# Loading V of a sliding-window attention in 18-token runs and transposing it twice

## The chip, the cores and the metric

The kernel runs on one core of a Trainium2 chip. The metric is the device time of one execution in microseconds (us), lower is better. A run counts as slow when it is over 1.5% above the fastest of the same kernel; every ratio below compares fast runs alone, while a median quoted is of all runs of a kernel, and where a slow one is among them this is said. A profile is of a single execution, and its span is about 1.8 us shorter than that execution's time. The profile of the kernel before (441.0 us) is of one of its faster runs.

## The reference

Eight batches of eight heads, 576 tokens, head size 64. Causal attention over the last 64 tokens, then a spectral mixing layer whose 64 modes each multiply by two 512 x 512 weight matrices, then a channel product with a residual.

```python
def _attn_ref(q, k, v):
    scores = scale * np.matmul(q, k.transpose(0, 1, 3, 2))
    mask = (rel >= 0) & (rel < 64)
    ...
    return np.matmul(attn, v)

def _moe_ref(x, w_r, w_i, w_ch):
    X = np.fft.rfft(x, axis=1)
    Yr = einsum('bmd,mde->bme', Xr, w_r) - einsum('bmd,mde->bme', Xi, w_i)   # 64 modes
    Yi = einsum('bmd,mde->bme', Xr, w_i) + einsum('bmd,mde->bme', Xi, w_r)
    y = np.fft.irfft(Y, n=S, axis=1); u = x + y
    return u + np.maximum(u @ w_ch, 0.0)
```

The 128 weight matrices (1 MB each in float32) are most of what has to be read.

## The kernel before

Three stages follow each other: attention, in 36 windows of 8 query blocks; the modes, which stream the weights; and the output tail. Weights are prefetched during attention. There are two kinds of prefetch. 19 "early" weights have buffers of their own and can be loaded at any time. 14 "spares" are loaded into attention's own buffers (raw K, Q, V, the transposed K and Q, the V tiles) when attention has used them for the last time.

```python
    def load_qk(b):
        rk = rawp.tile([128, 2, RUN * D], BF16, name="rk")      # RUN = 18 tokens; rawp has 2 buffers of each
        rq = rawp.tile([128, 2, RUN * D], BF16, name="rq")
        for r, src in ((rk, k), (rq, q)):
            nc.gpsimd.dma_start(out=r, in_=src[b].rearrange("(x g) (p c) d -> (g p) x (c d)", g=4, c=RUN))

    def load_v(b):
        rv = rawp.tile([128, 9, 4, D], BF16, name="rv")
        vf = v[b].rearrange("(hp hl) t d -> hp (hl t) d", hl=2)
        for hp in range(4):                                     # four loads of 4-token runs
            nc.gpsimd.dma_start(out=rv[32 * hp:32 * hp + 32, ...].rearrange("r j c d -> r j (c d)"),
                                in_=vf[hp].rearrange("(j r c) d -> r j (c d)", j=9, r=32))
    # ... in transpose_units(b):
        def vpart(a, j0, j1):                                   # selection matmuls: V onto key partitions
            ...
            for c in range(4):
                for i in range(2):
                    hp = 2 * a + i; pp = slice(32 * hp, 32 * hp + 32)
                    nc.tensor.matmul(out=pss[i][:, 0:n, :], lhsT=pick[pp, c, :],
                                     rhs=rv[pp, j0:j1, c, :], start=(c == 0), stop=(c == 3))
            ...
        return [vpart(0, 0, 5), part(rk, kT, 0, True), part(rk, kT, 6, False),
                vpart(0, 5, 9), part(rk, kT, 12, True), part(rq, qT, 0, True),
                vpart(1, 0, 5), part(rq, qT, 6, False), part(rq, qT, 12, True),
                vpart(1, 5, 9)]
    # ... the attention loop: three units of batch b in each of four windows
        def unit(b, j):
            ...
            if j == NU - 1:                                     # all units of batch b are traced
                if b + 2 < B:
                    load(b + 2)                                 # K, Q, V of batch b + 2
                early(2)                                        # the next two early weights
                if b >= B - 2:
                    early(EARLY); spare_raw()
```

Each engine works its instructions off in a fixed order. On PE that order is the program's (it is pinned there); on the other engines the framework's scheduler chooses it when the kernel is built. All loads are issued by POOL, in one such order, and each waits for its buffer, so a load that waits holds up every load behind it.

The softmax here doesn't subtract the row's maximum and nothing guards it: scores larger than these inputs give would overflow.

## Time and profile before

The median was 444.94 us (442.81 to 447.34, 4 runs).

From the page of the kernel before: each row has 40 slices of the span, 11 us each. PE is the busy share in tenths, PEclk the granted clock of PE in tenths, DMA the busy share of the DMA engines, GB/s what they wrote.

```profile
span 441.0 us, 11418 instructions
...
PE   6999999948998665122268886988576685899994
...
PEclk9999999986998555555558899686765856699998
DMA  8999999999999999999999999999999999991787
GB/s 138 196 207 209 213 209 208 212 209 213 209 213 214 214 214 232 238 214 209 197 213 202 213 202 211 212 214 214 213 213 214 215 213 213 213 189 40 246 301 273
```

From the third slice to the 35th the rate stays between 197 and 215 GB/s, mostly at 208 or more; the one rise, to 238, is the load of w_ch, which keeps its four bytes. Loads cast float32 to bf16, so twice that is read. PE is nearly always busy in the first 12 slices (attention), about a third idle in the middle (modes wait for weights; 128 of the 200 us between 180 and 380 us are busy), busy again at the end (tail). So the DMA stream decides when the modes end, and PE decides the tail.

The same by stage (the busy microseconds of each engine in each stretch, then PE's granted clock, DMA share and GB/s; the DMA share sums the times of packets, and here it passes 1):

```profile
core 0: us, PE busy (x) PEld busy (x) DVE busy (x) ACT busy (x) POOL busy (x), PEclk, DMA share, GB/s
12.00:100.00 88.00, 77.61 (x1533) 46.90 (x1533) 52.88 (x103) 55.17 (x103) 32.50 (x53) 0.98 1.16 208
100.00:150.00 50.00, 44.05 (x798) 26.74 (x801) 24.67 (x48) 25.31 (x48) 11.75 (x21) 0.84 1.10 212
...
180.00:380.00 200.00, 127.97 (x1656) 94.35 (x1657) 61.80 (x128) 29.50 (x59) 40.69 (x77) 0.69 1.06 211
```

From the page's groups of instructions and its DMA issues (KB each, us from issue to landing):

```profile
L105 POOL DMA_DIRECT2D rv<-in_v_dram x32 | 20.0, 628 | 20.3 <-DMA wt<-in_moe_w_i_dram 5.0
...
L238 PEld LDWEIGHTS <-pick 32*128 32x128 bf16 x256 | 10.8, 93 | 15.4 <-DMA rv<-in_v_dram 6.8
...
rk<-in_k_dram POOLq DMA_DIRECT2D x8, 576.0 KB, 11.8
...
rv<-in_v_dram POOLq DMA_DIRECT2D x32, 144.0 KB, 11.3
```

V takes 32 issues of 144 KB where K takes 8 of 576 KB, and the selection weights are loaded into PE 256 times. From POOL's timeline, the loads of batch 4 (start, duration, and what ended the idle time before):

```profile
start us, us, engine line op out<-in xcount [idle before <-releaser]
41.93 0.73 POOL L97 DMA_DIRECT2D rk<-in_k_dram  x1 [6.57 <-PE pst L223]
42.65 0.56 POOL L121 DMA_DIRECT2D wt<-in_moe_w_i_dram  x1
43.20 0.54 POOL L121 DMA_DIRECT2D wt<-in_moe_w_r_dram  x1
46.34 0.71 POOL L97 DMA_DIRECT2D rq<-in_q_dram  x1 [2.59 <-PE pst L223]
47.64 2.46 POOL L105 DMA_DIRECT2D rv<-in_v_dram  x4 [0.60 <-PE psv_1054 L238]
```

K of batch 4 is issued at 41.93 us, Q at 46.34, V at 47.64. Three early weights were issued earlier, two stand between K and Q. PE first works on them at 64.3 us. From 20 us to the end of attention PE waits for a load for more than 1 us only once, for V of batch 6 (us in total, times, longest):

```profile
engine line waited for: us in total, times, longest us
PE psv_2252 L238 <- DMA rv<-in_v_dram: 6.7, 1, 6.7
```

### The profile page before, as it was taken

How to read it: one execution, taken by the hardware profiler on the slowest of the kernel's cores; microseconds unless marked ns; L12 is line 12 of the kernel's file. 1: busy time of each engine (PE TensorE's matmuls, PEld its weight loads, DVE VectorE, ACT ScalarE, POOL GpSimd, SP SyncE). 2: the span in 40 equal slices, each digit the busy share in tenths (PEclk: the TensorE clock that was granted, in tenths of full speed). 3: DMA queues.
4: the chain of work that ended last, by engine and by line, in shares of the span. 5: the costliest groups of instructions: out<-in, count | busy, mean ns of one | idle time of the engine just before them, and what ended most of it. 6: DMA issues, size and time to landing. Idle time of an engine off the chain costs nothing.

```text
span 441.0 us, 11418 instructions
## 1 busy us (share of the span) xinstructions
PE 328.7 (75%) x4989; PEld 218.9 (50%) x5002; DVE 187.8 (43%) x393; ACT 141.4 (32%) x269; POOL 129.2 (29%) x217
## 2 busy tenths in 40 slices
PE   6999999948998665122268886988576685899994
PEld 2455656525565565122146665755344353555552
DVE  6475666633764103108612323221134433345774
ACT  4566767733764001001113232222110110104553
POOL 8642442323121322101212112121122122113484
PEclk9999999986998555555558899686765856699998
DMA  8999999999999999999999999999999999991787
GB/s 138 196 207 209 213 209 208 212 209 213 209 213 214 214 214 232 238 214 209 197 213 202 213 202 211 212 214 214 213 213 214 215 213 213 213 189 40 246 301 273
DMA packets 38338, 92.49 MB, mean 210 GB/s; under 512 B 3472, under 2 KB 12688, under 8 KB 38288
## 3 DMA queue, kind: packets, MB, share of 16 engines
q0 software_dynamic: 33040, 82.32, 96.7%
q1 hardware_dynamic: 5248, 9.44, 6.0%
q8 instruction: 39, 0.64, 0.5%
q14 instruction: 11, 0.09, 0.1%
HBM read 163.58 MB, written 9.44 MB: 392 GB/s over the span
## 4 chain that ended last, share of the span: by engine, by line
DMA 46%; PE 28%; issue 18%; POOL 3%; ACT 3%; DVE 1%; POOLq 0%; ACTq 0%
DMA wt<-in_moe_w_r_dram 31%; DMA wt<-in_moe_w_i_dram 11%; DMA rv<-in_v_dram 4%; PE pso L318 3%; POOL wt L121 3%; PE psc L727 2%; PE pss_212 L378 2%; PE pst L223 2%; PE psu L745 2%; PE psx L340 2%; PE psy L505 1%; PE psy L500 1%; PE psc L733 1%; PE psu L740 1%; ACT et L300 1%
## 5 line engine op out<-in xcount | busy, mean ns | idle before, releaser
L505 PE MATMUL psy<-XQ,wt 128*128 128x16 bf16 x912 | 56.2, 191 | 47.1 <-DMA wt<-in_moe_w_i_dram 47.0
L500 PE MATMUL psy<-XQ,wt 128*128 128x16 bf16 x912 | 58.1, 191 | 34.6 <-DMA wt<-in_moe_w_r_dram 29.8
L121 POOL DMA_DIRECT2D wt<-in_moe_w_i_dram x57 | 30.7, 538 | 178.1 <-PE psy L505 154.6
L505 PEld LDWEIGHTS <-wt 128*128 128x128 bf16 x912 | 43.8, 104 | 58.4 <-DMA wt<-in_moe_w_i_dram 56.9
L500 PEld LDWEIGHTS <-wt 128*128 128x128 bf16 x912 | 44.3, 104 | 45.7 <-DMA wt<-in_moe_w_r_dram 36.3
L543 DVE CAST xT<-pxt 128x512 fp32r<-128x512 bf16 x36 | 23.4, 687 | 67.4 <-PE pxt L540 67.4
L546 PE MATMUL psz<-wch,xT 128*128 128x512 f32 x144 | 47.7, 477 | 1.0 <-DVE xT L543 1.0
L548 ACT CAST Z_3232<-psz 128x512 fp32r<-128x512 f32 x36 | 21.1, 587 | 76.0 <-PE psz L546 76.0
L121 POOL DMA_DIRECT2D wt<-in_moe_w_r_dram x57 | 30.9, 541 | 37.7 <-PE psy L505 13.9
L666 DVE TENSOR_TENSOR Z_3232<-pse,Z_3232 128x512 fp32r<-128x512 f32 x36 | 23.7, 688 | 34.0 <-PE pse L644 33.4
L546 PEld LDWEIGHTS psz<-wch,xT 128*128 128x128 f32 x144 | 30.4, 224 | 7.2 <-issue 0.8
L318 PEld LDWEIGHTS <-et 128*64 128x64 bf16 (+1 forms) x576 | 22.8, 111 | 14.8 <-issue 8.3
L755 POOL TENSOR_TENSOR ot<-ot,r 128x512 f32<-128x512 f32 x18 | 22.8, 1286 | 23.2 <-ACT Yb_5588 L59 13.3
L326 DVE TENSOR_TENSOR x_sb<-pso,rcp 128x640 bf16<-128x640 f32 x32 | 26.3, 822 | 0.9
L105 POOL DMA_DIRECT2D rv<-in_v_dram x32 | 20.0, 628 | 20.3 <-DMA wt<-in_moe_w_i_dram 5.0
L60 DVE CAST YT<-psy 128x256 fp32r<-128x256 f32 x6 | 2.5, 423 | 53.2 <-PE psy L505 53.2
L748 ACT ACTIVATE r<-psc 128x512 f32<-128x512 f32 x36 | 19.0, 601 | 10.2 <-PE psc L733 9.6
L238 PEld LDWEIGHTS <-pick 32*128 32x128 bf16 x256 | 10.8, 93 | 15.4 <-DMA rv<-in_v_dram 6.8
L59 ACT CAST YT<-psy 128x256 fp32r<-128x256 f32 x6 | 2.2, 374 | 49.5 <-DVE YT L60 49.5
L318 PE MATMUL pso<-vt_204,et 128*64 128x65 bf16 (+1 forms) x288 | 17.1, 204 | 0.0
L300 ACT ACTIVATE et<-pss_211 128x512 bf16<-128x512 f32 x24 | 14.3, 597 | 7.4 <-PE pss_212 L294 7.4
L318 PE MATMUL pso<-vt_205,et 128*64 128x65 bf16 (+1 forms) x288 | 16.1, 208 | 0.5 <-DVE x_sb L326 0.5
(334 smaller groups left out, 631.9 us busy)
## 6 DMA issues: line engine op xcount, KB each, us to landing
wt<-in_moe_w_r_dram POOLq DMA_DIRECT2D x57, 512.0 KB, 10.6
wt<-in_moe_w_i_dram POOLq DMA_DIRECT2D x57, 512.0 KB, 8.6
out_dram<-ot SPq DMA_DIRECT2D x32, 256.0 KB, 2.3
rk<-in_k_dram POOLq DMA_DIRECT2D x8, 576.0 KB, 11.8
rq<-in_q_dram POOLq DMA_DIRECT2D x8, 576.0 KB, 13.3
rv<-in_v_dram POOLq DMA_DIRECT2D x32, 144.0 KB, 11.3
qT<-in_moe_w_r_dram POOLq DMA_DIRECT2D x2, 512.0 KB, 12.4
wch<-in_moe_w_ch_dram POOLq DMA_DIRECT2D x1, 1024.0 KB, 19.5
```

The costliest lines, as they stand in the source:

```text
L105: nc.gpsimd.dma_start(out=rv[32 * hp:32 * hp + 32, :, :, :].rearrange("r j c d -> r j (c d)"), in_=vf[hp].rearrange("(j r c) d -> r j (c d ...
L121: nc.gpsimd.dma_start(out=wt, in_=src[m].rearrange("(p c) e -> p c e", c=NC))
L318: nc.tensor.matmul(out=pso[po, hh, (i // 2) * VW:(i // 2) * VW + D + 1], lhsT=et[pk, hh, col:col + 64], rhs=vt[pk, 1 - f % 2, 2 * hh + g / ...
L326: nc.vector.tensor_tensor(out=view(x_sb, b * NT * DM + g * D, [[4 * D, 2], [DM, NT], [1, D]]), in0=view(pso, 0, [[512, 2], [VW, NT], [1, D]]),
L500: nc.tensor.matmul(out=psy[:, m % MG, e, :], lhsT=wr[:, c, ee], rhs=XQ[:, c, :, 1:3, m], start=(c == 0), stop=False)
L505: nc.tensor.matmul(out=psy[:, m % MG, e, :], lhsT=wi[:, c, ee], rhs=XQ[:, c, :, 0:2, m], start=False, stop=(c == NC - 1))
L543: nc.vector.tensor_copy(out=xT, in_=pst)
L546: nc.tensor.matmul(out=psz, lhsT=xT[:, c, :], rhs=wch[:, c, :], start=(c == 0), stop=(c == NC - 1))
L548: nc.scalar.copy(out=channel_out(i), in_=psz)
L666: nc.vector.tensor_tensor(out=channel_out(i), in0=ps, in1=channel_out(i), op=ALU.add)
L748: nc.scalar.activation(out=r, in_=psc, func=ACT_F.Relu)
L755: nc.gpsimd.tensor_tensor(out=ot, in0=ot, in1=r, op=ALU.add)
```

## The change

Intent: V comes in the same long runs as K and Q (2304-byte packets instead of 512), one load per batch instead of four. PE then transposes V like K (first round, written back over K's raw tile, whose K has been used by then) and once more per 128 keys (the way back), which puts keys on partitions.

```diff
+    def load_raw(b, r, src):
+        nc.gpsimd.dma_start(
+            out=r, in_=src[b].rearrange("(x g) (p c) d -> (g p) x (c d)", g=4, c=RUN))
+
     def load_v(b):
-        rv = rawp.tile([128, 9, 4, D], BF16, name="rv")
-        vf = v[b].rearrange("(hp hl) t d -> hp (hl t) d", hl=2)
-        for hp in range(4):
-            nc.gpsimd.dma_start(...)
+        rv = rawp.tile([128, 2, RUN * D], BF16, name="rv")
+        load_raw(b, rv, v)
@@ (the pick tiles of the selection are gone)
-        def vpart(a, j0, j1):
-            ... (selection matmuls)
+        def vback(u):
+            def f():
+                ps = ps_misc.tile([128, 6, 128], BF16, name="psv", tag="misc")
+                for i in range(6):
+                    ...
+                    for r0, n, g, t0 in parts:
+                        nc.tensor.transpose(out=ps[r0:r0 + n, i, :],
+                                            in_=view(rk, g * S + t0, [[1, n]]), identity=ident_bf)
+                evac(view(vt, 6 * u * VW, ...), view(ps, 0, ...), u != 1)
+                if u:
+                    ... (the shifted copies of V, as before)
@@
-        return [vpart(0, 0, 5), part(rk, kT, 0, True), ... vpart(1, 5, 9)]
+        return [part(rk, kT, 0, True), part(rk, kT, 6, False), part(rk, kT, 12, True),
+                part(rv, rk, 0, False), part(rv, rk, 6, True), part(rv, rk, 12, False),
+                part(rq, qT, 0, True), part(rq, qT, 6, False), part(rq, qT, 12, True),
+                vback(0), vback(1), vback(2)]
@@ ... NU = 12 units instead of 10
```

More of the change, by code (lines that the diff above doesn't have):

```diff
@@ L96, in load_qk @@
         for r, src in ((rk, k), (rq, q)):
-            nc.gpsimd.dma_start(
-                out=r, in_=src[b].rearrange("(x g) (p c) d -> (g p) x (c d)", g=4, c=RUN))
+            load_raw(b, r, src)
         raws[b] = [rq, rk]
+    def load_raw(b, r, src):
+        nc.gpsimd.dma_start(
+            out=r, in_=src[b].rearrange("(x g) (p c) d -> (g p) x (c d)", g=4, c=RUN))
     def load_v(b):
-        rv = rawp.tile([128, 9, 4, D], BF16, name="rv")
-        vf = v[b].rearrange("(hp hl) t d -> hp (hl t) d", hl=2)
-        for hp in range(4):
-            nc.gpsimd.dma_start(
-                out=rv[32 * hp:32 * hp + 32, :, :, :].rearrange("r j c d -> r j (c d)"),
-                in_=vf[hp].rearrange("(j r c) d -> r j (c d)", j=9, r=32))
+        rv = rawp.tile([128, 2, RUN * D], BF16, name="rv")
+        load_raw(b, rv, v)
         raws[b].append(rv)
@@ L167 @@
     nc.vector.tensor_copy(out=ident_r, in_=ident)
-    pick = acons.tile([128, 4, 128], BF16, name="pick")
-    nc.vector.memset(pick, 0.0)
-    for hp in range(4):
-        pp = slice(32 * hp, 32 * hp + 32)
-        nc.gpsimd.affine_select(out=pick[pp], in_=pick[pp], compare_op=ALU.not_equal, fill=1.0,
-                                base=0, pattern=[[-1, 4], [1, 128]], channel_multiplier=-4)
     NEG = -30000.0
@@ L228, in part @@
             return f
-        def vpart(a, j0, j1):
+        def vback(u):
             def f():
-                n = j1 - j0
-                pss = [ps_misc.tile([128, 5, D], FP32, name=f"psv{i}", tag="misc") for i in range(2)]
-                for c in range(4):
-                    for i in range(2):
-                        hp = 2 * a + i
-                        pp = slice(32 * hp, 32 * hp + 32)
-                        nc.tensor.matmul(out=pss[i][:, 0:n, :], lhsT=pick[pp, c, :],
-                                         rhs=rv[pp, j0:j1, c, :], start=(c == 0), stop=(c == 3))
-                for i in range(2):
-                    evac(vt[:, 0, 2 * a + i, j0:j1, 0:D], pss[i][:, 0:n, :], i == 0)
-                if j1 == 9:
-                    hs = slice(2 * a, 2 * a + 2)
+                ps = ps_misc.tile([128, 6, 128], BF16, name="psv", tag="misc")
+                for i in range(6):
+                    a, j = divmod(6 * u + i, 9)
+                    if j == 4:
+                        parts = [(0, 64, 2 * a, 512), (64, 64, 2 * a + 1, 0)]
+                    else:
+                        parts = [(0, 128, 2 * a + (j > 4), 128 * j - (j > 4) * S)]
+                    for r0, n, g, t0 in parts:
+                        nc.tensor.transpose(out=ps[r0:r0 + n, i, :],
+                                            in_=view(rk, g * S + t0, [[1, n]]), identity=ident_bf)
+                evac(view(vt, 6 * u * VW, [[18 * VW, 2], [VW, 6], [1, D]]),
+                     view(ps, 0, [[D, 2], [128, 6], [1, D]]), u != 1)
+                if u:
+                    hs = slice(u - 1, u + 2, 2)
                     nc.vector.tensor_copy(out=vt[64:128, 1, hs, 1:9], in_=vt[64:128, 0, hs, 0:8])
@@ L246, in vpart @@
             return f
-        return [vpart(0, 0, 5), part(rk, kT, 0, True), part(rk, kT, 6, False),
-                vpart(0, 5, 9), part(rk, kT, 12, True), part(rq, qT, 0, True),
-                vpart(1, 0, 5), part(rq, qT, 6, False), part(rq, qT, 12, True),
-                vpart(1, 5, 9)]
+        return [part(rk, kT, 0, True), part(rk, kT, 6, False), part(rk, kT, 12, True),
+                part(rv, rk, 0, False), part(rv, rk, 6, True), part(rv, rk, 12, False),
+                part(rq, qT, 0, True), part(rq, qT, 6, False), part(rq, qT, 12, True),
+                vback(0), vback(1), vback(2)]
     def head_of(n):
@@ L373, in spare_raw @@
         spare(rawp.tile([128, 2, RUN * D], BF16, name="rq"))
-        spare(rawp.tile([128, 9, 4, D], BF16, name="rv"))
+        spare(rawp.tile([128, 2, RUN * D], BF16, name="rv"))
     def warm_up(n):
@@ L384 @@
         first = transpose_units(0)
-        for i, j in enumerate((1, 2, 4, 5, 7, 8, 0, 3, 6, 9)):
+        for i, j in enumerate((0, 1, 2, 6, 7, 8, 3, 4, 5, 9, 10, 11)):
             first[j]()
@@ L392 @@
         early(1)
-        NU = 10
+        NU = 12
         sched = {}
@@ L397 @@
             start = -(-9 * (b - 1) // 2)
-            order = (1, 2, 4, 5, 7, 8, 0, 3, 6, 9) if b == 1 else range(NU)
-            for i, j in enumerate(order):
+            for i, j in enumerate(range(NU)):
                 sched.setdefault(start + i // 3, []).append((b, j))
```

## The prediction

> **What bounds the kernel.** The DMA stream. The page's DMA row reads about nine tenths from 11 us to 390 us, at 213 GB/s written; the chain of waits is 46% DMA. Loads cast float32 to bf16, so 426 GB/s are read; the Trainium skill (page "DMA: Bandwidth & Descriptors", section "Where 436 GB/s comes from") has 435 as ceiling; the trace agrees. So time = bytes / 213 GB/s + any time the DMA engines idle + a PE-bound tail of about 50 us. Before, they hardly idle: attention's PE (95% busy) waits once, 7 us at 93.5 us, for V of batch 6; 19 early weights, then 14 into freed attention buffers ("spares") keep the queue full; modes start at 148.8 us, the last spare lands at 156.
>
> **Saves.** No bytes. V's packets grow from 512 B to 2304 B. In 2 us slices of the DMA records V runs at 193 GB/s, K and Q at 208-211: over 4.7 MB about 2.1 us (estimate). Fewer DMA issues on POOL (0.63 us each) and no pick tiles (2.8 us) let K of batch 1 issue earlier: 0.5 us. On PE, 32 selection matmuls per batch (four groups of 0.45-0.6 us) become 36 transposes (0.35-0.5 us per 12) and 20 for the way back: about equal, as are ACT and DVE.
>
> **Costs.** rk now holds V's first round, so it is free for batch b+2 only in the fourth window of batch b, not the second. In POOL's instruction order, before, batch 4's loads stand after 3 to 5 early weights; after, 18 of the 19 precede batch 4's K, and batches 5, 6, 7 follow almost without weights. In queue order that is 18.3 MB through batch 4's K, which before's cumulative bytes reach at 93 us, less 2 us saved: K lands at 91-92 us. PE would be ready at about 64. So:
> - PE stalls before batches 2 and 3 (5-9 us each) and 4 (about 15), DMA still full.
> - From 92 us attention runs at PE's pace (14.4 us per batch, ACT timeline), and the loads for batches 6, 7 and the spares wait for buffers that PE frees. A batch loads in 8.4 us but is released every 14.4; DMA idles in part from 105 to 150 us. My tally of the order with these durations (estimate; giving 154 us for before's last spare, measured 156) has 20 us of DMA idle and the last spare at 171 instead of 154.
> - After before's 7 us stall the clock was granted at half for 10 us, costing about 2 us. The Trainium skill (page "TensorE: Matmul & The Clock Gate", Part 1) ties this to idleness. Add 2 us.
> The DMA-bound mode stage and the tail don't change, so the delay stays.
>
> **Sum.** 445.5 + 17 (savings inside) + 2 = about 464 us; range 456-470. Chances: faster 0.01, same 0.08, slower 0.91.
>
> **Would show it.** No 512 B packets; PE idle between 35 and 92 us, waiting for K; clock 0.5 there; GB/s under 190 between 105 and 150 us, POOL waiting on PE; modes starting at 166-170 us; the rest as long as before.
>
> **Would make it wrong.** If after's attention windows are clearly shorter than before's, part of the idle goes; if V's packets cost more than the dips show (summed packet time over 16 engines: 34.6 us, at K's rate 25), the saving could reach 8 us; slack in the mode stage would absorb some.

## The result

The changed kernel took 467.91 us (median; 466.66 to 473.23, 4 runs) against 444.94. The ratio is 1.0536, 95% interval 1.0462 to 1.0611: slower. A ratio here is the mean time of one kernel's fast runs over that of the other's in the same rounds, so it isn't quite the ratio of the medians quoted.

The page of the changed kernel, the same rows:

```profile
span 465.9 us, 11716 instructions
...
PE   6895958299899968623228869888666676899992
...
PEclk9997979589999775555557899877865756599997
DMA  8999999998856999999999999999999999981785
GB/s 148 213 213 214 212 214 213 211 184 130 141 94 114 188 174 214 213 256 214 213 213 213 210 214 206 213 212 213 214 214 214 213 213 213 213 165 46 250 310 209
```

From the second slice to the eighth the rate is 211 to 214 GB/s, better than before (196 to 213), though PE has holes in slices 4, 6 and 8, with a lowered clock. In slices 9 to 15 the DMA stream falls to 94 to 188 GB/s. By stage:

```profile
core 0: us, PE busy (x) PEld busy (x) DVE busy (x) ACT busy (x) POOL busy (x), PEclk, DMA share, GB/s
12.00:100.00 88.00, 64.60 (x1179) 41.13 (x1178) 39.02 (x65) 41.87 (x67) 17.09 (x28) 0.83 1.09 213
100.00:150.00 50.00, 47.67 (x1034) 31.82 (x1028) 34.20 (x59) 36.71 (x62) 6.96 (x11) 1.00 0.73 121
...
180.00:380.00 200.00, 127.31 (x1963) 98.36 (x1959) 59.70 (x155) 31.03 (x63) 41.30 (x79) 0.69 1.06 215
```

Between 100 and 150 us, 121 GB/s instead of 212. After 180 us the two kernels are alike (215 and 211). How many bytes had landed by when, counted from the packets of the two traces (us from the span's start; not a view of the profile):

```
MB landed       3.54   7.08  18.28  24.10  31.46  40.00  82.30   end
before          21.7   38.8   92.9  121.1  156.0  194.0  397.1  441.0
after           20.6   37.3   90.4  126.1  178.9  216.9  419.7  465.9
after - before  -1.0   -1.4   -2.6   +5.0  +22.9  +22.9  +22.6  +24.9
```

18.28 MB is everything through batch 4's K in the changed kernel's order; 31.46 MB is all of K, Q, V and the 33 prefetched weights. So: 2.6 us gained until 90 us, 25.5 us lost between 90 and 179 us, nothing more until the last weight, and 2.3 us lost after it.

POOL's timeline shows the order. Six weights stand between batch 3's K (issued at 43.47 us) and batch 4's V:

```profile
start us, us, engine line op out<-in xcount [idle before <-releaser]
...
45.27 0.55 POOL L120 DMA_DIRECT2D wt<-in_moe_w_r_dram  x1 [1.10 <-DMA wt<-in_moe_w_i_dram]
47.71 0.53 POOL L120 DMA_DIRECT2D wt<-in_moe_w_i_dram  x1 [1.89 <-DMA wt<-in_moe_w_r_dram]
50.12 0.53 POOL L120 DMA_DIRECT2D wt<-in_moe_w_r_dram  x1 [1.89 <-DMA wt<-in_moe_w_i_dram]
52.91 0.53 POOL L120 DMA_DIRECT2D wt<-in_moe_w_i_dram  x1 [2.25 <-DMA rv<-in_v_dram]
55.56 0.53 POOL L120 DMA_DIRECT2D wt<-in_moe_w_r_dram  x1 [2.12 <-DMA wt<-in_moe_w_r_dram]
58.20 0.53 POOL L120 DMA_DIRECT2D wt<-in_moe_w_i_dram  x1 [2.11 <-DMA rq<-in_q_dram]
61.27 0.70 POOL L101 DMA_DIRECT2D rv<-in_v_dram  x1 [2.54 <-DMA wt<-in_moe_w_i_dram]
...
66.19 0.70 POOL L101 DMA_DIRECT2D rq<-in_q_dram  x1 [2.19 <-PE pst L213]
...
71.10 0.70 POOL L101 DMA_DIRECT2D rk<-in_k_dram  x1 [2.18 <-PE pso L310]
...
100.49 0.72 POOL L101 DMA_DIRECT2D rv<-in_v_dram  x1 [18.52 <-PE pst L213]
```

K of batch 4 is issued at 71.10 us instead of 41.93 and, with a full queue ahead of it, lands 20.08 us later (the chain of waits has this piece), at 91.2 us. POOL in turn has issued K of batch 5 at 81.25 us and then waits 18.52 us for V of batch 6, whose buffer PE frees only when it has transposed V of batch 4. The waits between 20 and 170 us, the lines that matter:

```profile
engine line waited for: us in total, times, longest us
...
POOL rv L101 <- PE pst L213: 24.2, 2, 18.5
...
PE pst L213 <- DMA rk<-in_k_dram: 19.3, 3, 9.0
...
POOL rv L120 <- PE pst L213: 15.4, 2, 9.7
...
```

PE waited 19.3 us in three times for K; POOL then waited for PE in turn, for V's buffer alone 24.2 us, and 15.4 us more for the spares that go into it. The DMA engines, which are what the kernel is bound by, are then partly idle (DMA share 0.73 between 100 and 150 us, against 1.10 before).

### The profile page after: what moved, and what is told of

Same layout as the page of the kernel before. It is cut to its first block, busy times and chain, and to the rows that moved or that the text cites. A ratio compares the mean times of both kernels' runs of the same rounds, so it can differ in the third digit from the quotient of the medians.

```text
span 465.9 us, 11716 instructions
## 1 busy us (share of the span) xinstructions
PE 342.5 (74%) x5168; PEld 229.9 (49%) x5168; DVE 191.6 (41%) x384; ACT 148.0 (32%) x261; POOL 112.1 (24%) x189
## 3 DMA queue, kind: packets, MB, share of 16 engines
q0 software_dynamic: 25488, 82.32, 90.4%
## 4 chain that ended last, share of the span: by engine, by line
DMA 41%; PE 28%; issue 19%; POOL 4%; DVE 4%; ACT 1%; POOLq 0%; ACTq 0%
DMA wt<-in_moe_w_r_dram 22%; DMA rk<-in_k_dram 13%; PE pso L310 4%; DMA wt<-in_moe_w_i_dram 3%; PE pst L213 3%; DMA rv<-in_v_dram 3%; POOL wt L120 3%; PE psx L332 3%; PE psy L496 2%; PE psc L718 2%; PE psy L491 2%; PE psu L736 2%; PE pss L267 2%; PE psv L230 2%; DVE x_sb L318 2%
## 5 line engine op out<-in xcount | busy, mean ns | idle before, releaser
L120 POOL DMA_DIRECT2D wt<-in_moe_w_i_dram x57 | 30.4, 533 | 182.5 <-PE psy L496 159.7
L539 ACT CAST Z<-psz 128x512 fp32r<-128x512 f32 x36 | 21.1, 586 | 74.9 <-PE psz L537 74.9
L292 ACT ACTIVATE et<-pss 128x512 bf16<-128x512 f32 x72 | 39.2, 600 | 14.6 <-PE pss L286 12.9
L657 DVE TENSOR_TENSOR Z<-pse,Z 128x512 fp32r<-128x512 f32 x36 | 23.6, 687 | 36.2 <-PE pse L635 34.9
L310 PE MATMUL pso<-vt,et 128*64 128x65 bf16 (+1 forms) x576 | 33.7, 208 | 4.5 <-DVE x_sb L318 4.3
L213 PE MATMUL pst<-ident_bf,rk 128*64 128x128 bf16 x288 | 14.4, 255 | 19.3 <-DMA rk<-in_k_dram 19.3
L213 PEld LDWEIGHTS <-rk 128*64 128x64 bf16 x288 | 11.0, 131 | 24.0 <-DMA rk<-in_k_dram 19.7
L267 PE MATMUL pss<-band,ident_bf 64*64 64x512 bf16 x160 | 21.6, 438 | 1.4 <-ACT et L292 1.4
L739 ACT ACTIVATE r<-psc 128x512 f32<-128x512 f32 x36 | 19.0, 601 | 10.2 <-PE psc L724 9.6
L60 DVE COPY rk<-pst 128x768 bf16<-128x768 bf16 x16 | 15.3, 957 | 15.4 <-PE pst L213 15.4
```

Of the source, the lines that this page charges most:

```text
L120: nc.gpsimd.dma_start(out=wt, in_=src[m].rearrange("(p c) e -> p c e", c=NC))
L213: nc.tensor.transpose(out=ps[64 * hh:64 * hh + 64, c, :], in_=src[:, hh, (c0 + c) * D:(c0 + c + 1) * D], identity=ident_bf)
L267: nc.tensor.matmul(out=pss[(2 * w + hh) % 3][64 * half:64 * half + 64, :], lhsT=ident_bf[pp, pp], rhs=view(band[pp], 128 * half, [[0, WIN ...
L292: nc.scalar.activation(out=et[:, hh, :], in_=pss[(2 * w + hh) % 3], func=ACT_F.Exp, scale=EX_SCALE)
L310: nc.tensor.matmul(out=pso[po, hh, (i // 2) * VW:(i // 2) * VW + D + 1], lhsT=et[pk, hh, col:col + 64], rhs=vt[pk, 1 - f % 2, 2 * hh + g / ...
L657: nc.vector.tensor_tensor(out=channel_out(i), in0=ps, in1=channel_out(i), op=ALU.add)
```

## The experiments

Three theories. A, as the prediction told it: K's raw buffer is held longer by V's first round, and that pushes the weights ahead. B: the order moves because V is one load instead of four, whatever is held. C: the order doesn't matter; attention's windows are longer because of V's new work on PE, ACT and DVE. The orders of the loads as built (w is an early weight; parts of one V load that stand together are written once), up to batch 4's K:

```
before          rk rq rv rk rq rv rk rq rv w rk rq rv w w rk
after           rk rq rv rk rq rv w w w rq w rv w rk w w w rv w rq w rk w w w w w w rv w rq w rk
load_only       rk rq rv rk rq rv rk w rq w w w rv w w rk w rq w w w rv w w w w w w w rk
hold_only       rk rq rv rk rq rv rk rq rv w rq rk rv w w w w w rq rk
before_hoisted  rk rq rv rk rq rv w w w w w rk rq rv w w w w w rk rq rv w w w w w w w w rk   (fixed by hand)
load_only_split as before
after_split     rk rq rv rk rq rv rk rq rv w rq rk rv w w rv rq rv rk
```

### load_only: the kernel before with V as one 18-token load

The selection matmuls then read the wrong tokens, so the result is wrong; sizes and releases are as before.

```diff
-        for hp in range(4):
-            nc.gpsimd.dma_start(out=rv[32 * hp:32 * hp + 32, ...], in_=vf[hp]...)
+        nc.gpsimd.dma_start(
+            out=view(rv, 0, [[RUN * D, 2], [1, RUN * D]]),
+            in_=v[b].rearrange("(x g) (p c) d -> (g p) x (c d)", g=4, c=RUN))
```

> The kernel before, with only V's load changed to one 18-token load per batch; the selection matmuls stay, so the numbers are wrong on purpose, and every buffer is released when it was before. Theory A, which the prediction told (K's buffer, held longer by V's first round, is what pushes the weights ahead of the loads): with no hold nothing moves, so the time is before minus the 2 to 3 us that V's larger packets save, about 442 us. Theory B (what moves the order is that V is one load instead of four; the built order of this kernel already has 17 weights ahead of batch 4's K): DMA idle of about 20 us between 100 and 155 us, last spare weight some 18 us later, about 463 us. Theory C (the windows are longer because of V's new work on PE, ACT and DVE, and the order does not matter): about 442 us, since that work is not here.

Measured: 470.13 us, ratio 1.0543 (1.0469 to 1.0617). The whole slowdown is here, without any transpose of V and without any longer hold. The GB/s row of its page:

```profile
GB/s 148 212 213 213 213 214 213 212 142 155 146 75 123 200 213 213 234 236 213 214 213 208 209 212 185 195 205 208 213 214 213 209 213 213 214 193 45 247 312 209
```

The same trough in slices 9 to 14 as in the changed kernel. A and C both fall as the explanation of the whole; nine windows take 28.9 us here, as before, and still the 24 us are lost. What PE waits for is now V, as V is loaded last:

```profile
PE psv L236 <- DMA rv<-in_v_dram: 23.7, 3, 11.8
```

### hold_only: the kernel before with K's buffer held to the fourth window

```diff
+                if a == 1 and j0:
+                    ph = ps_misc.tile([128, 6, 128], BF16, name="psh", tag="misc")
+                    nc.tensor.transpose(out=ph[0:64, 0, :], in_=rk[:, 0, 0:D], identity=ident_bf)
+                    hold = small.tile([64, 1], BF16, name="hold")
+                    nc.vector.tensor_copy(out=hold, in_=ph[0:64, 0, 0:1])
```

(Added in `vpart`, ahead of its evacuations.)

> The kernel before, with one added transpose of K's raw tile (result unused) in the last V unit of each batch, so that K's buffer is released as late as in the changed kernel; loads and V work as before, output right. Theory A: the delay comes with the hold, about 460 us or more. Theory B: the built order keeps batch 4's K after 6 weights, so there is little DMA idle (estimate 3 to 6 us) and the time is 446 to 452 us. Theory C: 445 us.

Measured: 447.85 us, output right, ratio 1.0047 (0.9991 to 1.0103): the same within 2%. In its page one slice of attention drops:

```profile
GB/s 139 192 208 208 213 208 212 210 209 210 209 154 202 214 212 214 258 214 213 215 213 207 214 205 204 198 214 213 212 214 214 213 194 214 213 203 31 242 307 274
```

The hold alone costs about 1% at most (the upper end of the interval): the stream loses about 4 us around 125 us (31.46 MB landed at 159.7 us instead of 156.0). The hold does move the order a little: 6 weights stand ahead of batch 4's K instead of 3, but not 18. A has fallen as the explanation of the 24 us.

### before_hoisted: the kernel before with 18 weights ahead of batch 4's K

```diff
-    with tc.manual_schedule(engines={mybir.EngineType.PE}):
+    with tc.manual_schedule(engines={mybir.EngineType.PE, mybir.EngineType.Pool}):
...
+        early(5)
         load(2)
-        early(1)
...
+                early({1: 5, 2: 8, 3: 1}.get(b, 0))
                 if b + 2 < B:
                     load(b + 2)
-                early(2)
```

> The kernel before with nothing changed but the order of its loads, fixed by hand to put 18 weights ahead of batch 4's K as the changed kernel does. Theories A and B both say that this order alone makes the delay: DMA idle of about 19 us, last spare weight near 173 to 176 us instead of 156, time 463 to 466 us. Theory C (longer windows are the cause): within 3 us of before, since the DMA queue stays full or the windows are as before.

Measured: 465.28 us, output right, ratio 1.0439 (1.0372 to 1.0505). Such an order alone, with the old loads, the old V work and the old releases, makes about four fifths of the slowdown (4.4% of 5.4%). It isn't the changed kernel's order entry for entry (see the list above), so the last fifth is not explained by it; POOL's longer drain, about 2.4 us in load_only (below), is one part:

```profile
GB/s 140 201 211 209 212 209 213 208 191 146 151 83 106 188 155 214 213 257 214 213 213 214 212 214 176 211 213 214 213 214 213 212 200 214 214 213 33 234 300 279
```

### load_only_split: load_only with V's load issued in four parts

```diff
-        nc.gpsimd.dma_start(
-            out=view(rv, 0, [[RUN * D, 2], [1, RUN * D]]),
-            in_=v[b].rearrange("(x g) (p c) d -> (g p) x (c d)", g=4, c=RUN))
+        vg = v[b].rearrange("(x g) (p c) d -> g p x (c d)", g=4, c=RUN)
+        for g in range(4):
+            nc.gpsimd.dma_start(out=view(rv[32 * g:32 * g + 32], 0, [[RUN * D, 2], [1, RUN * D]]), in_=vg[g])
```

> As load_only (the kernel before with V loaded in 18-token runs, selection matmuls kept, numbers wrong on purpose), but V's load is issued in four parts of 32 partitions. The built order of loads is then the kernel before's, entry for entry. Theory B: 24 us come back and what is left is the saving of the larger packets alone, 2 to 3 us: about 0.994 of before. If the one load were slow for another reason than order (its packets, its landing), this stays above 455 us.

Measured: 446.27 us (wrong again), ratio 1.0018 (0.9956 to 1.0079). The same bytes in packets of the same length, in four issues instead of one: the built order is before's again, and the 24 us are gone.

```profile
GB/s 143 202 212 212 208 212 212 213 211 212 214 206 212 213 214 256 216 214 214 210 201 211 210 206 201 204 209 213 215 213 213 213 214 213 212 116 99 235 315 203
```

The expected saving of 2 to 3 us was missed. The stream is ahead of before by 1.6 us at 24.1 MB, when all of V has landed, and by 1.4 us at 82.3 MB (395.7 us). But in this profile the very last packets come late, so that the last weight lands only 0.1 us earlier than before; 1.2 us more are lost between the modes and the tail and 2.6 us after the last output is issued; see the drain below.

### after_split: the changed kernel, V's load issued in four parts

The diff is the one above, on `load_v` of the changed kernel.

> The changed kernel, V's load issued in four parts of 32 partitions and nothing else; no order is fixed by hand. The built order has batch 4's K after 3 early weights again and eight weights behind batch 7. Theory B: no stall of PE for K, a few us of DMA idle (estimate 6, from batch 2 and 4 waiting for buffers held by V's first round, and from longer windows): 444 to 450 us. Theory A (the hold makes the order): about 465 us.

Measured: 450.0 us (449.65 without the one slow run of six, which the ratio leaves out), output right, ratio 1.0103 (1.0044 to 1.0163). Splitting the load into four recovers about 19 of the 24 us with no order fixed by hand. In the profile, which is of a run of 453.96 us, most of what is lost is DMA idle between 44 and 70 us (15 MB landed at 82.9 us instead of 77.4): in this order the loads that wait for held buffers stand early, with no weight between them to fill in. So it seems that the hold does cost something once the order is good; that was argued from the order, not tested.

### after_pinned and after_tuned: the changed kernel with an order fixed by hand

POOL's order is pinned too, V, Q and K of batch b + 2 are loaded as soon as each buffer's last user is traced, and the early weights are spread (`GAP`) so that batch 4's K comes after 5 of them as built (the expectation says 6). after_tuned puts three weights ahead of batch 2's loads, where before one stood behind them, and takes two out of `GAP`; batch 4's K then comes after 6.

```diff
+        GAP = {1: (0, 0, 2), 2: (1, 1, 1), 3: (1, 1, 2), 4: (2, 1, 1), 5: (2, 1, 2)}     # after_pinned
+        def after_unit(b, j):                       # called at the end of unit(b, j)
+            if j not in (5, 8, 11):
+                return
+            i = (5, 8, 11).index(j)
+            name, src = (("rv", v), ("rq", q), ("rk", k))[i]
+            if b + 2 < B:
+                r = rawp.tile([128, 2, RUN * D], BF16, name=name)
+                load_raw(b + 2, r, src)
+                raws.setdefault(b + 2, [None] * 3)[(2, 0, 1)[i]] = r
+                early(GAP[b][i])
+            else:
+                spare(rawp.tile([128, 2, RUN * D], BF16, name=name))
```

> The changed kernel with nothing changed but the order of its loads, fixed by hand to spread the early weights as before did (batch 4's K after 6 weights). Theories A and B: the stalls for K go and DMA is full again: 442 to 447 us, the last spare weight landing at 153 to 157 us. The windows' extra time (about 8% over before's) should show as a few us of DMA idle at the end of attention at most. Theory C: the windows are still long, attention ends late, and the time stays above 455 us.

Measured: 448.61 us, output right, ratio 1.0057 (1.0002 to 1.0113), a little above the 442 to 447 us expected. C falls again as the main cause: the new V work is all there, and about 21 of the 24 us are gone. Its GB/s row still dips twice:

```profile
GB/s 145 177 203 211 213 213 213 211 212 214 215 192 197 196 193 214 258 214 214 213 214 203 214 188 211 213 215 212 214 214 214 207 210 214 213 155 86 244 311 206
```

In slice 2 POOL waits 11.9 us for K's buffer of batch 0 to be released, which V's first round holds; in slices 12 to 15 the spares wait for attention, whose windows are longer.

> The changed kernel with its order of loads fixed by hand, as after_pinned, with two more weights ahead of batch 2's loads, so that the queue has work while K's buffer of batch 0 is still held. Estimate from the order: the 1.6 us of idle at 20 us goes, about 3 us of idle before the last spares stay because the windows are longer: 443 to 447 us, 2 us better than after_pinned.

Measured: 446.0 us, output right, ratio 1.0009 (0.9959 to 1.006). The first dip is gone (3.54 MB at 20.7 us instead of 22.2). The stream is 2.5 us ahead of before at 24.1 MB, and 1 us behind at 31.46.

### after_tuned_nofill: without the filler matmuls

```diff
-                mask(w + 1, max(1, 3 - n))
+                mask(w + 1, 1)
```

> after_tuned, and the causal band is added once per window instead of up to three times (the repeats only keep PE busy). If the windows are long because PE's work grew (V's way back: 20 transposes at about 0.1 us, where I had counted half), taking away about 0.9 us of filler per nine windows gives 3 to 4 us of attention back: attention ends earlier, the idle before the last spares shrinks, 441 to 445 us. If the windows are set by ACT and DVE chains, or if the clock drops without the filler, no gain or a loss of a few us.

Measured: 452.88 us (451.94 without the one slow run of six, which the ratio leaves out), output right, ratio 1.0147 (1.0086 to 1.0208): unclear by the 2% rule, but slower than after_tuned, whose six runs, of the same rounds, are all faster than any of these. It is a miss, the other way. The PE clock row of this kernel's page:

```profile
PEclk9998996995996555555558888885865666799996
```

It drops in slices 4, 7 and 10: the clock records have half speed from 37.0 us for 3.4 us, from 71.2 for 6.8 and from 101.9 for 10.2. In after_tuned the first such record starts at 130.9 us. So in this kernel the filler is worth its time, some 1.4%. That the lowered clock is the reason is likely but not shown: before_early_end (below) keeps all its filler, its profile has 27.3 us at half clock in attention, and its stream is only 0.5 us behind before's at 31.46 MB. Its clock row:

```profile
PEclk9999966995999555555559887989565656699999
```

### after_tuned_early_end and before_early_end: a shorter end for POOL

In the trace's records (not in a view, which leave such instructions out) POOL ends with a drain instruction. In every kernel with V in 18-token runs it took over twice as long:

```
                     drain starts  takes   ends    output drained (SP)
before                    435.5     3.25   438.7   440.2
hold_only                 439.4     3.17   442.6   444.1
before_hoisted            460.4     3.42   463.8   465.1
after                     458.0     7.18   465.2   462.8
load_only                 458.5     7.18   465.7   463.3
load_only_split           436.5     7.34   443.8   441.3
after_tuned               436.1     7.18   443.2   440.8
after_tuned_early_end     435.1     7.24   442.4   442.2
```

Where it takes 7.2 us it ends 2.4 us after the output is done, and the kernel with it. The edit takes POOL's additions out of the last group of output tiles:

```diff
-                    group(h, [(b, t) for b in bs], (1, 3) if t else (3,))
+                    group(h, [(b, t) for b in bs], range(4) if h and t == NT - 2 else (1, 3) if t else (3,))
```

> after_tuned, and the last group of output tiles adds its residual in PE and DVE alone, so that POOL's last addition comes about 6 us earlier. In every kernel so far with V in 18-token runs the POOL drain after its last addition took 7.2 to 7.3 us, against 3.2 to 3.4 in the four with the old loads, and ended 2.4 us after the output had been drained. If the drain's length counts from POOL's last instruction and it alone holds up the end, 2.3 us go: about 443.5 us, 0.995 to 0.997 of before. If the drain is as long as it is because of something at the end of the program, it still ends last and nothing is gained (446 us).

Measured: 445.09 us, output right, ratio 1.0006 (0.9943 to 1.0068). (Of the old loads only three kernels had been traced when the expectation spoke of four.) The drain does count from POOL's last instruction: it still takes 7.24 us and now ends with the output. But the gain is not in the time. The end comes 4.4 us after the last output issue instead of 6.2, while the mode stage took 2 us more in this profile (82.3 MB at 399.5 us instead of 397.4). Inconclusive for the time.

> The same change of the last group on the kernel before. Its drain took 3.25 us and ended 1.4 us before the output had been drained, so by either reading nothing is gained there: 444.5 to 446.5 us, the 0.4 us of added PE work included.

Measured: 446.63 us, output right, ratio 1.0017 (0.9961 to 1.0074): nothing gained, as expected.

### in_place_spread: V's first round in V's own tile

V's three first-round blocks are all transposed before the first is written back over the raw V; K's buffer is then free after the second window, and one way-back unit stands in each of three windows. Order pinned and end shortened as above.

```diff
+        def vfirst():
+            pv = [ps_misc.tile([128, 6, 128], BF16, name="psr", tag="misc") for _ in range(3)]
+            ... (36 transposes of rv into pv, then three evacuations into rv)
...
-                                            in_=view(rk, g * S + t0, [[1, n]]), identity=ident_bf)
+                                            in_=view(rv, g * S + t0, [[1, n]]), identity=ident_bf)
...
+        return [vfirst, lambda: None, part(rk, kT, 0, True),
+                vback(0), part(rk, kT, 6, False), part(rk, kT, 12, True),
+                vback(1), part(rq, qT, 0, True), part(rq, qT, 6, False),
+                vback(2), part(rq, qT, 12, True), lambda: None]
```

> after_tuned_early_end, but V's first round is written back into V's own raw tile, so that K's is free again after the second window, and the three way-back units stand in three windows instead of all in the fourth. If the windows are long because DVE's V copies stand together in front of the normalisation that frees the output accumulator, they shorten by some 0.3 us of 3.4 and the idle before the last spares (3 us) shrinks: 441 to 443 us. If PE's own work sets them (94% busy), nothing moves: 443 to 445 us; V's three PSUM tiles at once could also stall PE and cost 1 to 3 us.

Measured: 442.3 us, output right, ratio 0.9934 (0.9881 to 0.9988): the same within 2%, but the interval lies below 1, so it is a little faster than the kernel before, and clearly than the changed one.

```profile
GB/s 143 213 213 211 201 211 213 213 212 214 214 213 214 214 214 239 233 214 193 210 212 194 211 208 204 212 212 214 213 213 214 214 213 214 213 193 36 253 293 282
```

No trough: 31.46 MB have landed at 154.2 us, 1.8 us earlier than before. Nine windows take 30.2 us, against 31.3 in after_tuned_early_end. Several things changed at once here, so the gain is shown for the sum only.

## Why the prediction was right, and where it was not

- **Bound by the DMA stream, and an idle stream is lost for good: right.** The lag of 22.9 us at 31.46 MB is still 22.6 us at the last weight, 240 us later. The mode stage had no slack.
- **Saves: right in kind, and the equal figures are luck.** 2.6 us were predicted in sum (2.1 for all eight loads of V, and 0.5); 2.6 us had been gained at 18.28 MB, but by then only five loads of V had landed, and 1.0 us of it was there at 3.54 MB already. load_only_split, with before's order, has the packets alone: 1.6 us at 24.1 MB, with all of V. Even there nothing was left in the time: late last packets, 1.2 us before the tail and 2.6 us of POOL's longer drain took more.
- **K of batch 4 at 91 to 92 us, PE stalling for batches 2, 3 and 4, POOL waiting for PE afterwards: right, the stalls too large.** K landed at 91.2 us, PE waited 5.1, 5.2 and 9.0 us (predicted 5 to 9 twice and about 15), and POOL's waits are where they were said to be. The modes started at 174.3 us, later than the 166 to 170 predicted.
- **"rk now holds V's first round, so it is free for batch b+2 only in the fourth window of batch b": this is the step that failed, as a cause.** The prediction read the new order from the build and put the hold in front of it as its reason. hold_only holds K's buffer just as long and keeps 447.85 us. load_only holds nothing longer and has the full 470.13 us. load_only_split differs from it in four issues instead of one and is at 446.27 us. The scheduler moved the weights because V became a single load. Why it does so is not shown by any run; that it does is. (Each of the four issues also waits only for the readers of its own 32 partitions; whether the number of issues or this finer wait decides was not separated.) The number did not suffer from the wrong cause, because it was worked out from the order as built.
- **"On PE ... about equal, as are ACT and DVE": mis-sized.** Nine windows (two batches) took 28.9 us before and 31.1 us after. The pattern of the windows repeats after nine, so nine of each are compared, not the same ones; busy time in the columns PE, PE weight load, DVE, ACT, POOL:

```profile
core 0: us, PE busy (x) PEld busy (x) DVE busy (x) ACT busy (x) POOL busy (x), PEclk, DMA share, GB/s
35.30:64.20 28.90, 27.58 (x588) 17.38 (x584) 19.42 (x38) 20.08 (x39) 10.10 (x17) 1.00 1.16 209
```

```profile
100.60:131.70 31.10, 29.28 (x630) 19.37 (x628) 20.93 (x37) 21.68 (x37) 4.28 (x7) 1.00 0.74 120
```

  PE is busy 1.7 us longer, DVE 1.5, ACT 1.6. Over the 20 windows from the stall to the end this is 4.9 us (20/9 of 2.2), which is about the size of the difference between the 19 us of delay predicted for the last spare weight (17 and 2) and the 22.9 measured. This is argued, not tested: load_only, with windows as short as before's, waits longer for data (23.7 us) and loses as much. Which of the three engines sets the pace was not settled.
- **The clock, +2 us: right in kind.** It was at half from 80.7 us for 17.1 us, around the stall for batch 4; what that cost was not isolated. The Trainium skill (page "TensorE: Matmul & The Clock Gate", Part 1) ties the lowered clock to idleness; the trace agrees in part: 1.0 and 0.5 are the only values, and two of the three drops began within a stall for K, but the third began 1.5 us before PE ran out of work at 82.2 us.
- **"The tail doesn't change": wrong by 2.3 us.** From the last weight to the end the span has 43.9 us before (441.0 - 397.1) and 46.2 after (465.9 - 419.7). It is POOL's drain.

Together: 24.9 us in the profiles = -2.6 (packets and earlier issue) + 25.5 (idle stream) - 0.3 (mode stage) + 2.3 (drain).

## What to carry to other kernels

When one queue feeds everything, the order in it is part of the design: compare the built order before and after any change to a load, even one that only merges four loads into one, and pin it if the stage depends on it. A prefetch that can go at any time is the filler for waits; if it is all spent early, the loads that must wait for a buffer have nothing to hide behind. And read a cause from an experiment, not from the diff: the part of the change that looks most like the culprit (here the held buffer) may be innocent of most of the loss.

## What the Trainium skill lacked or had wrong

- No page tells of a drain of several microseconds on POOL at the end of a program: 3.2 to 3.4 us in the kernels with 33,040 packets on the software queue, 7.2 to 7.3 us in those with 25,488 or 25,872, counted from POOL's last instruction. What sets it stays open.
- "DMA: Bandwidth & Descriptors", Specifications, gives 512 B as the least transfer for line rate. Here, in 2 us slices before 80 us, packets that write 512 B (V; 1024 B read) ran at 193 GB/s written, against 208 to 210 for 2304 B and 209 to 213 for 4096 B (medians): near line rate, not at it.
- "TensorE: Matmul & The Clock Gate", Part 4, says that transposes don't bring PE to full clock. No run here tests transposes alone, so this is open: in the stretch from 100.6 to 131.7 us, with transposes in most windows among other matmuls, the granted clock was 1.00, and the way-back transposes of 128 x 128 followed each other at a median of 57 ns there.
- "TensorE: Matmul & The Clock Gate", Part 1, gives one idle window of about 3.4 us as enough to lower the clock. These traces record drops without one: in the 3.4 us ahead of the three drops of after_tuned_nofill PE's longest idle was 1.2, 1.2 and 0.5 us, and before_early_end's drop of 17.1 us at 58.0 us follows 3.4 us in which PE was 83% busy and idle for 0.6 us at most. The lengths agree: without the filler 3.4, 6.8 and 10.2 us, multiples of about 3.4.
